# Gate and Up of two token tiles as seven products of 256 columns a pair of blocks, with sums of the weights kept in DRAM

## Chip, cores and metric

One core of one Trainium2 chip runs the whole kernel. The metric is the device time of one execution in microseconds (us); lower is better. TensorE (PE, with its weight loads shown as PEld), VectorE (DVE), ScalarE (ACT) and GpSimd (POOL) each run their own queue of instructions; SyncE (SP) issues nearly all transfers. Line numbers (L1059) are those of the kernel before.

## What is computed

x has 2048 tokens of 512 numbers. Both halves of the work start from the layer-normed x:

```
xn = layernorm(x)
s  = attention(xn)          # 32 heads of 16, causal window of 256 keys, then @ wo
h  = silu(xn @ w1) * (xn @ w3)     # 512 -> 1792, Gate and Up
g  = silu(h @ w2)                  # 1792 -> 512, Down
out = x + s * g
```

Results are wanted at nearly float32 accuracy. Every matrix is therefore scaled by a power of two and split into two float16 parts, high and low, and a product a @ b is computed as three: high x high, low x high, high x low.

## The kernel before

**Tiles.** Tokens go in four tiles of 512 (t = 0 to 3). The 1792 columns of w1 and w3 go in 14 blocks f of 128, in seven pairs j = (2j, 2j + 1). `X[t]` holds the normed tokens of a tile, turned so that the 512 features lie on the partitions in four pieces c, as XH (high) and XL (low).

**Gate and Up.** `gate_up(t, f)` makes Gate (k = 0, from w1) and Up (k = 1, from w3) of one block: for each k, 4 pieces x 3 products = 12 matmuls of 512 columns at L1059, added up in one PSUM bank. ACT takes tanh of Gate's bank (L1074), DVE multiplies it with Gate's bank (L1078, silu by way of tanh) and then with Up's bank (L1083). In tile 0 the weights are scaled and split as they come (`measure`, `split_pool`: two ACT instructions and four of POOL at L345 a weight) and their two parts are stored in `dW1`; later tiles load them from there (`load`), two blocks ahead.

**Down.** In tiles 0 and 1 h is split by ACT (L1092) and POOL (L339) and multiplied as it is (`down`, L1284). In tiles 2 and 3 Down already goes by Strassen's algorithm: `fold_first` and `fold_second` form sums of quarters of h (even and odd tokens by blocks 2j and 2j + 1) on POOL (L1116, L1117, L1125, L1140 to L1142) and ACT (L1114); `fold_down_piece` makes seven products of 256 columns (L1202), which ACT or DVE take out of PSUM (L1216, L1220); `unfold` adds them up to the four blocks of Down's result. The sums of w2 are made in tile 1 (`fold_weights`, L1014 to L1030) and kept in `dFold` (L1035).

**Attention.** 32 units (tile, group of 8 heads, half). Of each, `pass1` finds the maxima of the scores (PE L671, DVE L685), `pass2` computes scores again, adds masks (DVE L766), takes exp (ACT L769) and multiplies with the values (PE L787). A unit's rows are cut into five batches (`PLAN`).

**Order.** PE keeps the order in which the program issues; the other engines' queues are ordered by priority, with `urgent` ahead. `feed_forward` writes one list of dense pieces (Gate, Up, Down, loads, preparation of weights), each with a cost; `more` hands every unit its share, beside projections (`project`, L601), values (`value`, L567) and the output product (`total`, L1336). `spread` puts the dense pieces between the unit's batches in proportion to cost. `step` counts pieces and batches; `later(n, f)` runs f n steps on. A group of pieces that `opening` joins isn't parted by other dense pieces.

**Memory.** PSUM has four banks for scores, two for attention's results, and two, m0 and m1, for all dense products: `bank` gives them in turn. SBUF has 54 slots of 2 KB a partition; `take` gives the one that has been free longest, `give(..., after=n)` returns one, to be preferred from n steps on. Transfers go through SP's queue in the order of issue, and an instruction there waits for its data and its slot.

## Time and profile before

| | |
|---|---|
| median of 3 runs | 803.87 us |
| lowest and highest | 803.73 and 803.97 us |
| span of the profiled execution, first to last instruction | 801.8 us |
| instructions | 23974 |
| bytes read from and written to HBM | 91.23 and 36.57 MB |
| transfers "slot<-dW" of 256 KB | 98 |

The profile is of one execution, and of that execution it gives the span alone; the 2.07 us between it and the median lie before the first and after the last instruction, or between executions. In the profile's lists of groups a row gives line, engine, operation, what it writes and reads, shapes and count; after the first bar the engine's busy time in us and the mean duration of one in ns; after the second the idle time before, and what ended it. In a timeline a row gives start and length in us. Durations of PE's matmuls overlap: the next one starts before the one before has left the array, so pace is read from start to start. In rows of one line the three numbers are the shortest, median and longest duration in ns.

### The profile page before, as it was taken

How to read it: one execution, taken by the hardware profiler on the slowest of the kernel's cores; microseconds unless marked ns; L12 is line 12 of the kernel's file. 1: busy time of each engine (PE TensorE's matmuls, PEld its weight loads, DVE VectorE, ACT ScalarE, POOL GpSimd, SP SyncE). 2: the span in 40 equal slices, each digit the busy share in tenths (PEclk: the TensorE clock that was granted, in tenths of full speed). 3: DMA queues.
4: the chain of work that ended last, by engine and by line, in shares of the span. 5: the costliest groups of instructions: out<-in, count | busy, mean ns of one | idle time of the engine just before them, and what ended most of it. 6: DMA issues, size and time to landing. Idle time of an engine off the chain costs nothing.

```text
span 801.8 us, 23974 instructions
## 1 busy us (share of the span) xinstructions
PE 791.1 (99%) x9181; PEld 403.8 (50%) x9181; DVE 623.0 (78%) x2005; ACT 393.9 (49%) x592; POOL 381.2 (48%) x746
## 2 busy tenths in 40 slices
PE   8999999999999999999999999999999999999997
PEld 4443445444454444444445444466544744466465
DVE  8887889778797778787888887776678876874537
ACT  6989777744355544344443344344434334444411
POOL 2355657633229435365442546330446276650770
PEclk9999999999999999999999999999999999999999
DMA  9987654636666565657555733665453553334431
GB/s 281 245 258 238 196 185 144 248 111 208 173 215 189 169 210 144 214 148 258 130 194 173 213 114 101 177 173 157 137 159 87 159 157 110 89 117 134 129 94 56
DMA packets 109858, 134.18 MB, mean 167 GB/s; under 512 B 18928, under 2 KB 64944, under 8 KB 109744
## 3 DMA queue, kind: packets, MB, share of 16 engines
q1 hardware_dynamic: 109456, 132.13, 55.4%
q8 instruction: 72, 1.18, 0.6%
q10 hardware_dynamic: 288, 0.52, 0.2%
q14 instruction: 42, 0.34, 0.1%
HBM read 91.23 MB, written 36.57 MB: 159 GB/s over the span
## 4 chain that ended last, share of the span: by engine, by line
PE 80%; DVE 8%; DMA 4%; ACT 3%; issue 2%; POOL 1%; SPq 1%; DVEq 0%; ACTq 0%; POOLq 0%
PE m L1059 31%; PE po L787 9%; PE m L601 8%; PE m L1202 8%; PE m L1284 7%; PE s L759 5%; PE m L1336 4%; PE m L567 4%; PE s L671 3%; DMA slot<-in_B_w_dram 2%; DVE junk L685 2%; PE po L671 2%; ACT sqa L249 1%; DVE s L766 1%; POOL slot L345 1%
## 5 line engine op out<-in xcount | busy, mean ns | idle before, releaser
L1059 PE MATMUL m<-XH,slot 128*128 128x512 f16 x896 | 267.3, 380 | 1.1 <-DVE slot L1078 0.6
L769 ACT ACTIVATE pt<-s,es 128x1024 f32<-128x1024 f32 x152 | 167.6, 1112 | 178.7 <-DVE s L766 176.9
L1059 PEld LDWEIGHTS <-slot 128*128 128x128 f16 x1344 | 124.9, 98 | 155.6 <-issue 13.1
L1059 PE MATMUL m<-XL,slot 128*128 128x512 f16 x448 | 169.8, 379 | 0.0
L766 DVE TENSOR_TENSOR s<-s,MK 128x256 f32<-128x256 f32 (+2 forms) x280 | 118.7, 434 | 53.5 <-PE s L759 49.8
L685 DVE CUSTOM_DVE_ANT_0 junk<-s,MW 128x320 bf16<-128x320 f32 x276 | 133.9, 485 | 18.4 <-PE s L671 11.4
L339 POOL TENSOR_TENSOR slot<-slot,slot 128x256 f16<-128x256 f32 (+1 forms) x86 | 57.6, 692 | 128.8 <-ACT slot L1092 60.0
L345 POOL TENSOR_TENSOR slot<-slot,slot 128x128 f16<-128x128 f32 x168 | 68.9, 444 | 76.6 <-ACT slot L343 76.6
L685 DVE CUSTOM_DVE_ANT_0 junk<-po,MW 128x320 bf16<-128x320 f32 x172 | 83.4, 485 | 4.6
L1284 PE MATMUL m<-slot,slot 128*128 128x512 f16 x336 | 78.5, 380 | 1.1 <-DVE slot L1078 1.1
L787 PE MATMUL po<-pt,V 64*32 64x320 f32 (+4 forms) x2880 | 77.2, 342 | 0.1
L601 PE MATMUL m<-XH,slot 128*128 128x512 f16 x240 | 70.8, 380 | 0.5 <-DVE slot L1078 0.5
L1202 PE MATMUL m<-slot,slot 128*128 128x256 f16 x588 | 68.4, 273 | 0.0
L1074 ACT ACTIVATE slot<-m,sgs 128x512 f32<-128x512 f32 x56 | 38.3, 684 | 59.8 <-PE m L1059 59.7
L1117 POOL TENSOR_TENSOR slot<-slot,slot 128x256 f16<-128x256 f32 x98 | 64.6, 671 | 1.1
L1202 PEld LDWEIGHTS <-slot 128*128 128x128 f16 x588 | 56.2, 98 | 11.5 <-issue 2.8
L787 PEld LDWEIGHTS po<-pt,V 64*32 64x32 f32 x2880 | 50.4, 106 | 22.4 <-issue 0.8
L1078 DVE SCALAR_TENSOR_TENSOR slot<-slot,m 128x512 f32<-128x512 f32 x56 | 38.3, 684 | 28.9 <-ACT slot L1074 26.7
L759 PE MATMUL s<-qa,KA 50*64 50x320 f16 (+3 forms) x1472 | 58.3, 259 | 0.0
L601 PEld LDWEIGHTS <-slot 128*128 128x128 f16 x392 | 36.5, 98 | 42.6 <-issue 1.7
L759 PEld LDWEIGHTS <-KA 50*64 50x64 f16 x1472 | 30.1, 105 | 51.7 <-issue 32.8
L1284 PEld LDWEIGHTS <-slot 128*128 128x128 f16 x336 | 30.7, 98 | 39.2 <-issue 4.7
(194 smaller groups left out, 1131.5 us busy)
## 6 DMA issues: line engine op xcount, KB each, us to landing
slot<-dW SPq DMA_DIRECT2D x98, 256.0 KB
slot<-in_B_w_dram SPq DMA_DIRECT2D x56, 256.0 KB
slot<-dFold SPq DMA_DIRECT2D x48, 256.0 KB
dW<-slot SPq DMA_DIRECT2D x42, 256.0 KB
slot<-in_A_x_dram SPq DMA_DIRECT2D x30, 256.0 KB
KA<-dK SPq DMA_DIRECT2D x24, 288.0 KB
slot<-dWQ SPq DMA_DIRECT2D x24, 256.0 KB
qa<-dQ SPq DMA_DIRECT2D x30, 192.0 KB
```

What stands on the lines that cost most here:

```text
L339: op(out[:, c], a[:, c], b[:, c])
L345: nc.gpsimd.tensor_sub(lo[:, c:c + P], raw[:, c:c + P], hi[:, c:c + P])
L601: nc.tensor.matmul(cell["pp"][:, cols[n]], w[:, (a * NC + c) * P:(a * NC + c + 1) * P], b[:, c, cols[n]], start=n == 0 and (c, i) == parts ...
L685: lasts["maximum"] = nc.vector.tensor_tensor_reduce(out=junk[:, :n], in0=s[:, r, :n], in1=mask, scale=1.0, scalar=NEG, op0=ALU.add, op1=AL ...
L759: nc.tensor.matmul(s[64 * h:64 * h + 64, r, o:o + 64 * n], ka[rows, 2 * p + a, 64 * (m + 4):64 * (m + 5)], qa[rows, 2 * p + a, 64 * (m + k ...
L766: nc.vector.tensor_add(v, v, MK[:, kind, of:of + n, :].unsqueeze(1).to_broadcast([P, 2 * len(which), n, 64]))
L769: lasts["exp"] = nc.scalar.activation(pt, s, AF.Exp, scale=es)
L787: nc.tensor.matmul(cell["po"][32 * i:32 * i + 32, h, 64 * (m + k):64 * (m + k + n)], V[64 * h:64 * h + 64, (4 * t + m // 2) % VB, hd * VW: ...
L1059: nc.tensor.matmul(cell[k], w[:, (a * NC + c) * P:(a * NC + c + 1) * P], b[:, c, :], start=c == 0 and i == 0, stop=c == NC - 1 and i == 2)
L1117: nc.gpsimd.tensor_sub(lo, view, hi)
L1202: nc.tensor.matmul(cell["ps"][:, c], made[:, f:f + P], wj[:, g:g + 256], start=j == j0 and c == 0 and n == 0, stop=j == j1 - 1 and n == 2, ...
L1284: nc.tensor.matmul(ps, hh[:, a * TW + b * P:a * TW + (b + 1) * P], w[:, c * D:(c + 1) * D], start=f == f0 and i == 0, stop=f == f1 - 1 and ...
```

## The change

For tiles 2 and 3, Gate and Up of a pair of blocks are computed by Strassen's algorithm (in Winograd's form of seven products). The tokens' features are cut into halves d = 0, 1 (pieces c = 0, 1 and 2, 3), the tokens into halves of 256, the weights' columns into the two blocks. A product now has 256 columns and 256 features, and Gate and Up of it share one PSUM bank (columns 0 to 255 and 256 to 511): 12 matmuls of 256 columns.

- `quad(t, j)` replaces `gate_up` for a pair: p1, p2, p6, p5, p7, p3, p4, in this order. p1, p6, p5 and p3 add up in one bank, which `retained` keeps from other use meanwhile; after each, ACT copies its state to SBUF (`copied`). p2, and p7 with p4, use the other bank; DVE adds those to a copy (`added`). From each finished quarter `activated` makes half of h: tanh on ACT, a product on DVE, and the product with Up on POOL.
- `weight_sums(j)` makes four sums of blocks a pair and weight (POOL), splits them and stores them in `dSum`; it is started at seven places of tiles 1 and 2 (`QUAD_AT`). `token_sums(t)` makes the tokens' sums, kept in SBUF (`HALF`), at `HALVES_AT`.
- `load_quad` loads seven slots of 256 KB a pair, issued beside the products of the quad before (`LOADS`).
- `split_blocks` lays high and low parts of w1 and w3 out by feature halves, so that a half with both parts is one piece of `dW1`; `gate_up` reads that layout. `by_half` parts tokens by halves and not by parity.
- Scales: XS and the scale of h in tiles 2 and 3 (HF) are halved, copies are scaled by CS.
- Order: `arranged` places the other dense runs around a quad's four runs (p1 p2, p6, p5 p7, p3 p4), with one other run after p6; pieces marked `glued` aren't parted by batches. Of Down's products of the fold before at most seven runs (`LATE`) follow each quad. Projections of one group and the totals of tile 2 move by a unit.

```diff
-XS = 2.0**10
+XS = 2.0**9
+HF = 2.0**3
+CS = 2.0**-21
+LATE = 7
+QUAD_FROM = 2
+QUAD_AT = ((1, 2), (1, 4), (1, 7), (1, 10), (1, 13), (2, 1), (2, 2))
+HALVES_AT = {2: (1, 8), 3: (2, 5)}
...
-        open_bank[0] = b = 1 - open_bank[0]
+        open_bank[0] = b = 1 - (open_bank[0] if retained[0] is None else retained[0])
...
+    def weight_sums(j):
...
+        def sums(k):
+            a, b = (cell["raw"][i][k] for i in range(2))
+            add(b[:, r], b[:, l], b[:, r])
+            sub(b[:, l], a[:, l], b[:, l])
+            sub(a[:, l], b[:, r], a[:, l])
+            sub(a[:, r], a[:, r], a[:, l])
+
+        def cut(i, k):
+            raw = cell["raw"][i][k]
+            made = take(F16)
+            with behind_exp():
+                nc.scalar.copy(made[:, 0:512], raw)
+            halves(sub, made[:, 512:], raw, made[:, 0:512])
...
+                    nc.sync.dma_start(dSum[i, k, j], made)
...
+        def product(ps, w, x, first):
+            for k in range(2):
+                for c in range(2):
+                    for n, (a, b) in enumerate(((0, 0), (1, 0), (0, 1))):
+                        nc.tensor.matmul(ps[:, 256 * k:256 * k + 256], w(k, a, c), x(b, c),
+                                         start=first and k == 0 and c == 0 and n == 0,
+                                         stop=k == 1 and c == 1 and n == 2, skip_group_check=True)
+
+        def copied(ps):
+            made = take(F32)
+            with urgent():
+                lasts["exp"] = nc.scalar.activation(made, ps, AF.Copy, scale=CS)
+            return made
+
+        def added(ps, other):
+            with urgent():
+                lasts["emptied"] = nc.vector.scalar_tensor_tensor(other, ps, CS, other, op0=ALU.mult, op1=ALU.add)
+            return other
+
+        def activated(f, half, made, done_with=True):
...
+            nc.scalar.activation(h, made[:, 0:256], AF.Tanh, scale=sg_apart[:, f:f + 1])
+
+            def gated():
+                nc.vector.scalar_tensor_tensor(h, h, 1.0, made[:, 0:256], op0=ALU.add, op1=ALU.mult)
+                nc.gpsimd.tensor_mul(h, h, made[:, 256:512])
+                give(made, after=10)
+            later(1, gated)
...
+        def p6():
+            product(cell["a"], summed_up(0, 0), token_sum(1, 256), False)
+            cell["u2"] = copied(cell["a"])
+
+        def p5():
+            product(cell["a"], summed_up(1, 256), token_sum(0, 0), False)
+            cell["v5"] = copied(cell["a"])
+
+        def p7():
+            cell["b"] = bank([P, 512])
+            product(cell["b"], summed_up(1, 0), token_sum(0, 256), True)
+            give(QW[t, j, 5], QW[t, j, 6])
+            activated(o, 1, added(cell["b"], cell["v5"]))
+
+        def p3():
+            product(cell["a"], summed_up(0, 256), tokens(1, 256), False)
+            give(QW[t, j, 3], QW[t, j, 4])
+            retained[0] = None
+            activated(e, 1, copied(cell["a"]))
+
+        def p4():
+            product(cell["b"], plain(2), token_sum(1, 0), False)
...
+            activated(o, 0, added(cell["b"], cell["u2"]))
...
+            later(2, lambda: fold(e, fold_first))
+            later(3, lambda: fold(o, fold_second))
...
+            if t >= QUAD_FROM:
+                for j in range(FB // 2):
+                    pieces += sums_of(t, j)
+                    if j == 0 and t > 2:
+                        pieces += soon
+                    pieces += quad(t, j)
+                    some, late = late_of(late)
+                    pieces += some
...
-            for u, half in ((max(2 * k - 5 + (k == NG), 0), 1), (2 * k - 4, 0)):
+            for u, half in ((max(2 * k - 5 + (k in (NG, 3 * NG)), 0), 1), (2 * k - 4, 0)):
...
-        b = n % 8 - (2 if t < 3 else 3)
+        b = n % 8 - (2 if t < 3 else 4)
```

More of the change, by code (lines that the diff above doesn't have):

```diff
@@ new lines, in tile_block, with token_sums, both, sums @@
+    HALF = {}
+    def token_sums(t):
+        assert turned[t] == 4
+        xh, xl = X[t]
+        add, sub = nc.gpsimd.tensor_add, nc.gpsimd.tensor_sub
+        l, r = slice(0, 256), slice(256, 512)
+        whole = [take(F32) for _ in range(NC)]
+        HALF[t] = [None] * NC
+        def both(c):
+            halves(add, whole[c], xh[:, c, :], xl[:, c, :])
+        def sums(c):
+            a, b = whole[c], whole[2 + c]
+            sub(a[:, l], a[:, r], a[:, l])
+            sub(a[:, r], b[:, r], a[:, r])
+            sub(b[:, r], b[:, r], a[:, l])
+            sub(b[:, l], b[:, l], b[:, r])
+        def cut(c):
+            HALF[t][c] = made = take(F16)
+            with behind_exp():
+                nc.scalar.copy(made[:, 0:512], whole[c])
+            halves(sub, made[:, 512:], whole[c], made[:, 0:512])
+            give(whole[c], after=20)
+        n = 0
+        for f, cs in ((both, (0, 2, 1, 3)), (sums, (0, 1)), (cut, (0, 2, 1, 3))):
+            for c in cs:
+                later(n, lambda f=f, c=c: f(c))
+                n += 2
@@ L1376, in total_by_columns, with is_open, in_groups @@
         give(y, xr)
+    def is_open(pieces):
+        return bool(pieces) and hasattr(pieces[-1][1], "opens")
+    def in_groups(pieces):
+        groups = []
+        for piece in pieces:
+            if groups and is_open(groups[-1]):
+                groups[-1].append(piece)
+            else:
+                groups.append([piece])
+        return groups
     def feed_forward():
@@ L1447, in tile_block @@
     done = [0]
-    def is_open(pieces):
-        return bool(pieces) and hasattr(pieces[-1][1], "opens")
-    def in_groups(pieces):
-        groups = []
-        for piece in pieces:
-            if groups and is_open(groups[-1]):
-                groups[-1].append(piece)
-            else:
-                groups.append([piece])
-        return groups
     def more(want):
@@ L1508, in spread, with in_runs @@
+    def in_runs(dense):
+        runs = []
+        for piece in dense:
+            if runs and getattr(runs[-1][-1][1], "glued", False):
+                runs[-1].append(piece)
+            else:
+                runs.append([piece])
+        return runs
     def spread(made, dense):
         whole = sum(c for c, _ in dense) + sum(c for c, _ in made)
-        dense = list(dense)
+        dense = in_runs(dense)
         at = 0
@@ L1516, in spread @@
             at += cost
-            while dense and (at + dense[0][0] / 2 <= whole * (k + 1) / len(made) or dense[0][0] == 0):
-                c, piece = dense.pop(0)
+            while dense:
+                c = sum(c for c, _ in dense[0])
+                if c and at + c / 2 > whole * (k + 1) / len(made):
+                    break
                 at += c
-                piece()
-                if c:
-                    step()
-        run(dense)
+                run(dense.pop(0))
+        run([piece for r in dense for piece in r])
     def run(dense):
@@ L1663, in tile_block @@
         mine = more(want)
-        lists = in_groups(beside[n]), in_groups(mine)
+        head = next((i for i, (_, f) in enumerate(mine) if hasattr(f, "quad")), len(mine))
+        groups = in_groups(beside[n])
+        part_of = 0
+        if head == len(mine):
+            part_of = len(groups)
+        elif any(c for c, _ in mine[:head]):
+            part_of = round(len(groups) * sum(c for c, _ in mine[:head]) / sum(c for c, _ in mine))
+        lists = groups[:part_of], in_groups(mine[:head])
         both = sorted([((i + 0.5) / len(l), k, i) for k, l in enumerate(lists) for i in range(len(l))])
-        spread(batches(n, u, units[n + 2] if n + 2 < len(units) else None), [piece for _, k, i in both for piece in lists[k][i]])
+        dense = [piece for _, k, i in both for piece in lists[k][i]]
+        if head < len(mine):
+            dense += arranged([piece for g in groups[part_of:] for piece in g], mine[head:])
+        spread(batches(n, u, units[n + 2] if n + 2 < len(units) else None), dense)
         k = n // 2 + 2
```

218 lines of the change are left out of this document (208 added, 10 removed).

## Prediction

> **What bounds the kernel now.** I read the page's first part, then the busy times by stretch, then the costliest groups, then the waits.
>
> ```profile
> PE 791.1 (99%) x9181; PEld 403.8 (50%) x9181; DVE 623.0 (78%) x2005; ACT 393.9 (49%) x592; POOL 381.2 (48%) x746
> ...
> DMA  9987654636666565657555733665453553334431
> ...
> PE 80%; DVE 8%; DMA 4%; ACT 3%; issue 2%; POOL 1%; SPq 1%; DVEq 0%; ACTq 0%; POOLq 0%
> ...
> core 0: us, PE busy (x) PEld busy (x) DVE busy (x) ACT busy (x) POOL busy (x), PEclk, DMA share, GB/s
> 220.00:430.00 210.00, 209.78 (x2521) 99.32 (x2518) 170.93 (x534) 100.19 (x133) 105.32 (x190) 1.00 0.61 187
> 430.00:773.00 343.00, 342.38 (x4327) 184.20 (x4320) 249.00 (x753) 138.12 (x179) 162.75 (x276) 1.00 0.48 136
> ```
>
> TensorE (PE) is busy 791.1 of 801.8 us, at full clock in every stretch (1.00), and holds 80% of the chain. From 430 to 773 us, where Gate and Up of tiles 3 and 4 lie, it is idle for 343.00 - 342.38 = 0.62 us. So time is won only by giving PE less to do, and lost by any new wait of PE. VectorE (DVE) is at 73% there, ScalarE (ACT) at 40%, GpSimd (POOL) at 47%: none bounds, but PE's PSUM banks are emptied by DVE and ACT.
>
> **What goes, on PE.** A pair of blocks f, f+1 now takes 2 x 2 x 12 = 48 matmuls of 512 columns at L1059; after, seven products of 12 matmuls of 256 columns, 84. Durations overlap, so I take start to start, at the tail where nothing lies between:
>
> ```profile
> 768.07 0.60 PE L1059 MATMUL m<-XH,slot 128*128 128x512 f16 x2
> ...
> 773.04 0.38 PE L1059 MATMUL m<-XL,slot 128*128 128x512 f16 x1
> 773.26 13.92 PE L1202 MATMUL m<-slot,slot 128*128 128x256 f16 x126
> ```
>
> 24 matmuls of L1059 start from 768.07 to 773.04: 4.97 / 23 = 216 ns each. The 126 of L1202 (the Down products, also 256 columns, each with its own weights) take 13.92 us, of which the last one's 0.273 is pipeline: 13.65 / 125 = 109.2 ns. A pair: 48 x 0.216 = 10.37 us before, 84 x 0.1092 = 9.17 after, 1.20 less; 7 pairs x 2 tiles: **-16.8 us**. This is the whole gain; nothing else leaves PE. The new scales, halves in place of parities and the other layout of w1 and w3 in `split_blocks` keep the counts and shapes of instructions, and projections and totals put a unit later move PE's work without changing it: nothing, hidden as now by PE's other dense work.
>
> **What comes, beside PE.** Prices from the groups (mean ns after the busy time):
>
> ```profile
> L1078 DVE SCALAR_TENSOR_TENSOR slot<-slot,m 128x512 f32<-128x512 f32 x56 | 38.3, 684 | 28.9 <-ACT slot L1074 26.7 <-DMA rb<-de 2.0
> L1083 DVE SCALAR_TENSOR_TENSOR slot<-m,slot 128x512 f32<-128x512 f32 x56 | 38.5, 687 | 13.9 <-PE m L1059 13.6
> L1074 ACT ACTIVATE slot<-m,sgs 128x512 f32<-128x512 f32 x56 | 38.3, 684 | 59.8 <-PE m L1059 59.7
> L343 ACT CAST slot<-slot 128x512 f16<-128x512 f32 x42 | 25.0, 611 | 0.5
> L342 ACT ACTIVATE slot<-slot,pi 128x512 f32<-128x512 f32 x28 | 19.4, 714 | 1.7 <-DVE pi L302 1.7
> L1114 ACT CAST slot<-slot 128x256 f16<-128x256 f32 x42 | 15.6, 403 | 59.9 <-DVE slot L1083 59.9
> L1220 DVE SCALAR_TENSOR_TENSOR slot<-m,fd,slot 128x512 f32<-128x512 f32 x14 | 10.5, 748 | 7.0 <-PE m L1202 6.8
> L1140 POOL TENSOR_TENSOR slot<-slot,slot 128x256 f32<-128x256 f32 x14 | 10.2, 727 | 53.7 <-DVE slot L1083 44.7 <-DVE NM L704 9.0
> L1216 ACT ACTIVATE slot<-m,fd 128x512 f32<-128x512 f32 x14 | 9.6, 686 | 21.1 <-PE m L1202 16.0 <-issue 5.0
> L339 DVE TENSOR_TENSOR slot<-slot,slot 128x256 f32<-128x256 f32 x6 | 2.3, 416 | 0.0
> ...
> L1117 POOL TENSOR_TENSOR slot<-slot,slot 128x256 f16<-128x256 f32 x98 | 64.6, 671 | 1.1
> q1 hardware_dynamic: 109456, 132.13, 55.4%
> ```
>
> DVE, a pair: 2 x (684 + 687) = 2.74 us go; three additions out of PSUM at 748 (L1220) and four half products at 416 (the 256-wide row of L339) come: 3.91. That is +1.2 a pair, 16 us in all. ACT: 2 x 684 goes; four copies at 686 (L1216) and four half activations at 403 (L1114, 256 wide) come: +3.0 a pair, 42 us. POOL: four products at 727, 2.9 a pair, 41 us. The sums of w1 and w3, once a pair, in the second tile and the start of the third: ACT 4 x 714 + 4 x 611 = 5.3, POOL 8 x 727 + 8 x 671 = 11.2, seven times 37 and 78 us. The token sums, twice: POOL 16 x 727 + 8 x 671 = 17 us. From 430 to 773, less the 17 us: DVE 265 of 326 (81%), ACT some 58%, POOL some 71%. None is full, so I put the busy time itself at nothing; it is hidden by PE's own 326 us, and costs where it makes PE's banks come free late.
>
> Transfers: 28 loads and 28 stores of 256 KB for the sums, and 98 loads for 56 in tiles 3 and 4, 25.7 MB more. By the q1 row 132.13 MB took 55.4% of 801.8 us, 3.36 us a MB. About 14 MB fall between 220 and 430: the share there goes from 0.61 to 0.83. The DMA row stands at 9 tenths in its first slices, so that much can be had. A quad's weights are asked for one quad (over 20 us) ahead, so I put transfers at nothing. All are issued by SP, in order, and a store waiting for POOL's cut holds everything behind it, the attention's fetches too. The nearest case is the folded w2's store:
>
> ```profile
> SPq L1035 <- POOL slot L1030: 9.2, 2, 8.8
> ```
>
> It held SP once for 8.8 us, between 220 and 430, where PE lost 0.22 us in all. A longer hold is in the range's upper part.
>
> **Term 1, hand-overs of PSUM banks.** `bank` has two banks. Before, each is filled for 12 matmuls of 512 (2.6 us) while the other is emptied. In a quad, bank a goes p1, p6, p5, p3, and each product adds onto what the one before left, after ACT has copied it; bank b goes p2, other work, p7, p4. So the cover is one product: p6 waits for the copy of p1 behind p2 alone, p3 for that of p5 behind p7, the next piece for that of p3 behind p4 (ACT, three); the middle piece for the addition of p2 behind p6, p4 for that of p7 behind p3, p7 for the middle piece's emptying behind p5, p2 for the piece before p1 (DVE, mostly, four). p5, which needs the copy of p6, has the middle piece before it. That is seven a quad, 98. Behind each, PE holds all scores, projections and products that follow, and DVE and ACT wait for those.
>
> ```profile
> 427.46 0.38 PE L1059 MATMUL m<-XL,slot 128*128 128x512 f16 x1
> 428.47 0.69 DVE L1083 SCALAR_TENSOR_TENSOR slot<-m,slot 128x512 f32<-128x512 f32 x1
> ...
> L1083 DVE SCALAR_TENSOR_TENSOR slot<-m,slot x28: 678/689/693, 428.5 to 773.5; 128x512 f32<-128x512 f32 x28
> ...
>   PE m L1059: 9.2, 10
> ...
> L1074 ACT ACTIVATE slot<-m,sgs x27: 679/687/688, 446.4 to 770.9; 128x512 f32<-128x512 f32 x27
> ...
>   PE m L1059: 38.4, 19
> ...
> 791.77 0.74 DVE L1340 SCALAR_TENSOR_TENSOR slot<-m,us,slot 128x512 f32<-128x512 f32 x1
> 792.56 2.75 PE L1336 MATMUL m<-slot,slot 128*128 128x512 f16 x12 [0.20 <-DVE slot L1340]
> ...
> 429.06 0.64 PE L759 MATMUL s<-qa,KA 50*64 50x320 f16 x24
> ```
>
> From the end of a product's last matmul the next product covers 13 x 0.1092 - 0.273 = 1.15 us. PE starts 0.05 after DVE's end (791.77 + 0.74 to 792.56). So the emptying may start 1.15 - 0.05 - 0.75 = 0.35 us late on DVE, 0.41 on ACT (0.69). How late does it start? In tiles 3 and 4, 28 rows of L1083 and 14 of L1220 start 0.31 us after their last matmul on average (the first of them 428.47 - 427.84 = 0.63); DVE was found idle for 10 of the 28. 17 of the 42 pass 0.35 us, by 0.13 a case over all 42. ACT (L1074, L1216; idle for 19 of 27) has a mean of 0.15, an excess of 0.04. Bare: 3 x 0.04 + 4 x 0.13 = 0.64 us a quad, 9.0 in all. But attention's batches go between the runs of a quad, five a unit, some 80 over 14 quads, and a batch adds at least 0.6 us of cover (0.64 in the row). With 0.6 more the same 42 leave 0.01 and 0.02: 1.6 in all. With all delays doubled and no batch (0.13 and 0.42), 29. I take **+5**, near the middle of 1.6 and 9.0, since runs and batches are about equal in number but not always alternate.
>
> **Term 2, POOL in the second tile.** POOL's 105 of 210 us gets six pairs' sums and one tile's token sums, 84: 90%. What PE needs from it there is the low half of h for Down (L339):
>
> ```profile
> 255.03 0.69 DVE L1083 SCALAR_TENSOR_TENSOR slot<-m,slot 128x512 f32<-128x512 f32 x1 [0.38 <-PE m L1059]
> ...
> 259.38 1.30 POOL L339 TENSOR_TENSOR slot<-slot,slot 128x256 f16<-128x256 f32 x2
> ...
> 263.45 1.46 PE L1284 MATMUL m<-slot,slot 128*128 128x512 f16 x6
> ```
>
> h is ready at 255.72, its low half at 260.68, and PE starts that group at 263.45: 2.8 us to spare, with POOL starting on it 3.7 us after h. A block of sums of one weight is 4 x 727 = 2.9 us ahead in POOL's queue. Between nothing and 2.9 for each of four groups (11.6); I take **+1.5**, since the bulk is not urgent and can go behind.
>
> **Term 3, the tail.** After the last product h passes addition, activation, product on DVE and on POOL by halves, 0.75 + 0.40 + 0.42 + 0.73 = 2.3 us, where one DVE operation (0.69) led to the fold before:
>
> ```profile
> 774.23 0.73 POOL L1140 TENSOR_TENSOR slot<-slot,slot 128x256 f32<-128x256 f32 x1 [4.48 <-DVE slot L1083]
> ...
> 780.69 1.41 POOL L339 TENSOR_TENSOR on<-on,rb 128x256 f32<-128x256 f32 x2
> ```
>
> POOL begins 1.6 us later and has two or three half products and the first fold in front, so the operand of the third Down product comes about 1.3 us late, and the attention's last product (780.69) 3 us, which has about 2 of slack. From 0 to 4; I take **+1.5**.
>
> **Sum.** -16.8 + 5 + 1.5 + 1.5 = -8.8. Against the profiled execution: 801.8 - 8.8 = 793.0 us of span; the median shown, 803.87, is 2.07 above that span, so 795.1. I say **795.0**. About 0.2% (1.6 us) is what a measurement of this kernel can tell from no change.
>
> **Rivals.** *Nearly the whole gain* (22%): batches shelter all hand-overs (1.6), POOL's order costs nothing, tail 0.5: 803.87 - 14.7 = 789.2. For it: PE loses only 0.62 in 343 us with DVE at 73%. Against: every cover there is twice as long.
>
> *Given back* (12%): bare hand-overs with delays half longer, some 13, and terms 2 and 3: 803 to 804.
>
> *VectorE becomes the late one, slower* (21%). Place: the four hand-overs emptied by DVE, and the half product `gated`, whose two inputs both lie in SBUF. Rows of that kind:
>
> ```profile
> 217.80 1.30 POOL L339 TENSOR_TENSOR slot<-on,slot 128x256 f16<-128x256 f32 x2
> ...
> 218.65 1.00 DVE L251 CUSTOM_DVE_ANT_0 junk<-slot 128x512 bf16<-128x512 f32 x1
> ...
> L334 DVE SCALAR_TENSOR_TENSOR slot<-slot,sw,slot x12: 739/747/910, 11.4 to 79.3; 128x512 f16<-128x512 f32 x12
> ...
> L251 DVE CUSTOM_DVE_ANT_0 junk<-slot x10: 676/686/1005, 16.6 to 225.2; 128x512 bf16<-128x512 f32 x10
> ```
>
> Their longest are 163 and 319 ns over their medians; the longest, at 218.65, begins while POOL works through two instructions (217.80 to 219.10). With POOL at 71%, 56 half products held for some 0.2 that often put 8 us on DVE: 273 of 326, 84%; the ratio of its busy to its idle time goes from 2.6 to 5.2, and its queue's delays about double. At 0.2 us over 98 hand-overs, 19.6 us, with terms 2 and 3 the time is 803.87 - 16.8 + 22.6 = 809.7. It decides from 0.14 (13.8 + 3 = 16.8). Against it: before 430 us DVE ran at 81% (170.93 of 210) and PE lost 0.22 us, under the longer cover. [...]
>
> *The change doesn't do what it says* (3%): 256-column products run slower than 109 ns since each needs its weights, or a store holds SP till weights are late. Each 5 ns a matmul is 1176 x 5 = 5.9 us; 126 in a row at 109.2 speak against it.
>
> **Chances.** Forecast 42%; it stands for 791 to 802. The last rival's 3% fall evenly on the three outcomes. Faster: 42 + 22 + 1 = 65%; same: 12 + 1 = 13%; slower: 21 + 1 = 22%. Range 787.5 (the whole gain, 787.1, with 0.4 lost) to 807.0, inside the slow rival, which leaves out about 3% below and 15% above.
>
> **What would show it.** Products' matmuls 109 ns apart; PE's idle time between 430 and the end of the last quad, now 0.62 us, at about 5, ended by copies and additions of the quads (right), near 1.6 (first rival) or near 20 with DVE over 84% (third). PE waits at Down in the second tile for POOL: term 2. A gap of one to two us between the last quad and the last Down products: term 3. I am wrong if the quads' matmuls are further apart, or if PE waits for a transfer.

## The result, and the profile after

The changed kernel takes 912.09 us (median of 4 runs, 908.82 to 914.71) against 803.92 for the kernel before in the same comparison (803.73 to 804.30): 1.134 times as long, 95% interval 1.131 to 1.137. The forecast of 795.0 and its whole range are missed. The profiled execution has a span of 907.0 us, 105.2 more than before. Line numbers from here on are those of the changed kernel, unless another is named.

The page's busy times, its chain and its clock row:

```profile
PE 802.7 (88%) x9685; PEld 462.6 (51%) x9685; DVE 642.3 (71%) x2048; ACT 464.4 (51%) x740; POOL 535.3 (59%) x962
...
PE 20%; POOL 9%; DVE 6%; issue 4%; ACT 3%; DMA 3%; SPq 1%; DVEq 0%; POOLq 0%; ACTq 0%
...
PEclk9999999999999989999998898899999999999999
```

(The chain's shares add up to 47% only, so it breaks off, and nothing is built on it here.) By its matmuls' pace TensorE was to have 16.8 us less work, and yet it is busy 802.7 us, 11.6 more than before; and it is idle for 907.0 - 802.7 = 104.3 us, where it was idle for 801.8 - 791.1 = 10.7. So 93.6 us of the loss is idle time, and the rest is longer busy time: 11.6 + 16.8 = 28.4 us. The last row explains most of that: the granted clock, 1.00 in every stretch before, has 8s in it, and its mean over the run is 0.966. In the trace's record of the clock every piece is full or half. The half pieces add up to 61.4 us inside the span, and PE was busy for 42.1 of them; matmuls of 256 columns start 213 ns apart there and 109 elsewhere (medians), so the cost is some 21.0 (an estimate: half of 42.1). The other 7.4 weren't measured apart. A likely part of them: PE stops 82 times, 23 times before, and at each stop the end of the last matmul is overlapped by no next one (an estimate: 59 stops at 379 - 216 = 163 ns are 9.6 us).

Busy time by stretch (columns as before: PE, PEld, DVE, ACT, POOL, then the clock):

```profile
220.00:430.00 210.00, 190.24 (x2224) 88.72 (x2229) 149.36 (x470) 109.02 (x153) 148.84 (x245) 0.97 0.65 192
430.00:600.00 170.00, 130.19 (x1746) 78.86 (x1731) 109.05 (x324) 73.24 (x114) 106.62 (x174) 0.90 0.55 165
600.00:873.00 273.00, 244.32 (x3393) 175.24 (x3391) 176.90 (x526) 125.10 (x191) 162.28 (x258) 0.97 0.54 158
```

The loss begins in the second tile, which has the sums' preparation and not one quad: PE lost 0.22 us there before and now 210.00 - 190.24 = 19.8. The worst stretch, 430 to 600, has quads and the last of the preparation together: 39.8 us idle, clock 0.90. DVE, ACT and POOL are all less loaded there (64, 43 and 63%) than DVE alone was before (73%).

The waits (engine, line, what it waited for; total, times, longest), first of the compute engines, then of SP's queue:

```profile
ACT slot L1135 <- POOL slot L1440: 55.6, 23, 5.2
PEld L618 <- DMA slot<-dWQ: 41.6, 9, 11.8
PE m L1414 <- ACT slot L1421: 19.0, 11, 6.4
```
```profile
SPq L1591 <- POOL slot L347: 13.5, 5, 10.5
SPq L1389 <- POOL slot L1440: 11.3, 4, 6.1
SPq L1387 <- PE m L1414: 7.6, 5, 3.8
```

Two chains stand behind these rows. **SP's queue.** The biggest wait of PE is for `dWQ`, the weights of the attention's projections (L618), which the change doesn't touch. The timelines of SP, POOL and PE about the longest case (start, length; SP's rows give when a transfer was issued):

```profile
554.58 0.46 SPq L1328 DMA_DIRECT2D dSum<-slot  x1
555.09 0.43 SPq L1387 DMA_DIRECT2D slot<-dW  x1
566.07 0.35 SPq L1591 DMA_DIRECT2D out_dram<-slot  x1
...
567.49 0.90 SPq L653 DMA_DIRECT2D slot<-dWQ  x2
...
562.69 0.74 POOL L1137 CAST slot<-slot 128x256 f16<-128x256 f32 x2
563.39 1.29 POOL L1138 TENSOR_TENSOR slot<-slot,slot 128x256 f16<-128x256 f32 x2
564.64 1.40 POOL L347 TENSOR_TENSOR slot<-slot,slot 128x256 f32<-128x256 f32 x2
...
559.02 0.31 PE L688 MATMUL s<-KA,qa 48*64 48x320 f16 x4
570.82 1.03 PE L618 MATMUL m<-XH,slot 128*128 128x512 f16 x2 [11.49 <-DMA slot<-dWQ]
571.65 0.63 PE L618 MATMUL m<-XL,slot 128*128 128x512 f16 x1
...
573.96 0.38 PE L618 MATMUL m<-XL,slot 128*128 128x512 f16 x1
```

After 555.5 us SP issues nothing until 566.07: there stands the store of a result (L1591), whose last addition is POOL's (L347, 564.64 to 566.04), and POOL comes to it only after folds, half products and sums. (It is the 10.5 us, the longest, of the row for L1591.) Behind the store wait two transfers, and then the two loads of `dWQ`, issued at 567.49. PE, which needs them, stands from 559.33 to 570.82. A store of a finished tile holds up the weights of an unrelated product. And when PE comes back, a matmul of 512 columns takes 0.63 us at 571.65 and 0.38 at 573.96: the clock had been halved meanwhile (by the trace's record at 563.46). The loads of the quads' weights hold SP in the same way, by L1389 for a slot that POOL has still to read, and by L1387 for one that PE is reading.

**ACT's queue.** The timelines of ACT and PE about another stop, at 682 us:

```profile
678.68 0.61 ACT L1370 CAST slot<-slot 128x512 f16<-128x512 f32 x1
682.39 0.40 ACT L1135 CAST slot<-slot 128x256 f16<-128x256 f32 x1 [3.09 <-POOL slot L1440]
682.70 0.50 ACT L1436 ACTIVATE slot<-slot,sga 128x256 f32<-128x256 f32 x1
683.11 1.09 ACT L786 ACTIVATE pt<-s,es 128x1024 f32<-128x1024 f32 x1
684.11 0.58 ACT L1421 ACTIVATE slot<-m 128x512 f32<-128x512 f32 x1
...
680.11 1.48 PE L1414 MATMUL m<-slot,slot 128*128 128x256 f16 x12
684.74 2.78 PE L1414 MATMUL m<-slot,slot 128*128 128x256 f16 x24 [3.15 <-ACT slot L1421]
```

The first instruction of the fold of h (L1135, a cast) reached the head of ACT's queue 3.09 us before POOL had finished the half product it reads (L1440). Behind it stand an activation, an exp and only then the copy of a PSUM bank (L1421), on which PE's next product waits for 3.15 us. ACT is busy for 46% of 600 to 873 us, but nothing in its queue passed that cast: the three behind it began at 682.70, 683.11 and 684.11. Altogether it stood at that cast for 55.6 us. Both chains are read from one case each; the runs below ask how much each is worth.

### The profile page after: what moved, and what is told of

It is laid out like the page before. It is cut to its first block, busy times and chain, and to the rows that moved or that the text cites. A ratio compares the mean times of both kernels' runs of the same rounds, so it can differ in the third digit from the quotient of the medians.

```text
span 907.0 us, 25623 instructions
## 1 busy us (share of the span) xinstructions
PE 802.7 (88%) x9685; PEld 462.6 (51%) x9685; DVE 642.3 (71%) x2048; ACT 464.4 (51%) x740; POOL 535.3 (59%) x962
## 5 line engine op out<-in xcount | busy, mean ns | idle before, releaser
L786 ACT ACTIVATE pt<-s,es 128x1024 f32<-128x1024 f32 x152 | 167.4, 1112 | 171.2 <-DVE s L783 163.7
L347 POOL TENSOR_TENSOR slot<-slot,slot 128x256 f16<-128x256 f32 (+1 forms) x158 | 105.2, 693 | 102.2 <-ACT slot L1113 47.2
L702 DVE CUSTOM_DVE_ANT_0 junk<-s,MW 128x320 bf16<-128x320 f32 x276 | 134.0, 485 | 29.9 <-PE s L688 22.4
L1414 PEld LDWEIGHTS <-slot 128*128 128x128 f16 x1176 | 115.3, 100 | 49.8 <-issue 30.5
L1080 PE MATMUL m<-XH,slot 128*128 128x512 f16 x448 | 133.7, 380 | 0.6 <-DVE slot L639 0.3
L618 PE MATMUL m<-XH,slot 128*128 128x512 f16 x240 | 77.4, 410 | 41.0 <-DMA slot<-dWQ 38.0
L1080 PEld LDWEIGHTS <-slot 128*128 128x128 f16 x672 | 62.1, 98 | 77.9 <-issue 6.7
L1414 PE MATMUL m<-slot,slot 128*128 128x256 f16 x672 | 84.4, 280 | 10.7 <-ACT slot L1421 6.9
L702 DVE CUSTOM_DVE_ANT_0 junk<-po,MW 128x320 bf16<-128x320 f32 x172 | 83.7, 487 | 4.7
L1080 PE MATMUL m<-XL,slot 128*128 128x512 f16 x224 | 84.9, 379 | 0.0
L618 PEld LDWEIGHTS <-slot 128*128 128x128 f16 x392 | 37.9, 103 | 91.0 <-DMA slot<-dWQ 41.6
L1440 POOL TENSOR_TENSOR slot<-slot,slot 128x256 f32<-128x256 f32 x56 | 41.5, 741 | 67.6 <-DVE slot L1439 36.9
L1223 PE MATMUL m<-slot,slot 128*128 128x256 f16 x588 | 69.7, 276 | 7.1 <-ACT slot L1237 2.9
L363 POOL TENSOR_TENSOR slot<-slot,slot 128x128 f16<-128x128 f32 x112 | 46.8, 452 | 47.8 <-DMA dQ<-slot 26.4
L1138 POOL TENSOR_TENSOR slot<-slot,slot 128x256 f16<-128x256 f32 x98 | 66.9, 692 | 11.7 <-ACT slot L1135 10.5
L1414 PE MATMUL m<-XH,slot 128*128 128x256 f16 x336 | 58.8, 279 | 13.1 <-ACT slot L1421 12.1
L1223 PEld LDWEIGHTS <-slot 128*128 128x128 f16 x588 | 56.5, 99 | 18.9 <-issue 8.9
L804 PEld LDWEIGHTS po<-pt,V 64*32 64x32 f32 x2880 | 52.4, 107 | 22.4 <-issue 2.9
```

What stands on the lines that cost most here:

```text
L347: op(out[:, c], a[:, c], b[:, c])
L618: nc.tensor.matmul(cell["pp"][:, cols[n]], w[:, (a * NC + c) * P:(a * NC + c + 1) * P], b[:, c, cols[n]], start=n == 0 and (c, i) == parts ...
L702: lasts["maximum"] = nc.vector.tensor_tensor_reduce(out=junk[:, :n], in0=s[:, r, :n], in1=mask, scale=1.0, scalar=NEG, op0=ALU.add, op1=AL ...
L786: lasts["exp"] = nc.scalar.activation(pt, s, AF.Exp, scale=es)
L804: nc.tensor.matmul(cell["po"][32 * i:32 * i + 32, h, 64 * (m + k):64 * (m + k + n)], V[64 * h:64 * h + 64, (4 * t + m // 2) % VB, hd * VW: ...
L1080: nc.tensor.matmul(cell[k], w[:, at:at + P], b[:, c, :], start=c == 0 and i == 0, stop=c == NC - 1 and i == 2)
```

## The experiments

Seventeen kernels were run, each beside the kernel before (803.9 to 804.9 in all comparisons). The expectations call the theories by letters: **Q**, queues run in order and SP or ACT stands at an instruction that waits for GpSimd; **S**, SBUF slots are short, so a load or a copy gets one that is still in use; **H**, hand-overs of PSUM banks, each covered by one product of 1.15 us only; **A**, of Q the part on ACT. Others are explained where they come. Times are medians; PE's idle time is the span less PE's busy time of the page, 10.7 us before.

| kernel | us | ratio, 95% interval | PE idle |
|---|---|---|---|
| changed kernel | 912.1 | 1.131 to 1.137 | 104.3 |
| e1 `dWQ` loaded earlier | 924.3 | 1.146 to 1.153 | 115.7 |
| e2 half product on DVE | 890.6 | 1.104 to 1.111 | 87.7 |
| e3 weights' sums not computed | 886.6 | 1.099 to 1.106 | 85.8 |
| e6 preparation moved | 901.0 | 1.115 to 1.125 | 100.1 |
| e7 e6 with e2 | 885.6 | 1.091 to 1.110 | 90.8 |
| e11 fold later | 903.8 | 1.121 to 1.127 | 92.0 |
| e4 preparation, no quads | 855.0 | 1.060 to 1.066 | 47.3 |
| e12 order and layout alone | 805.6 | 1.001 to 1.003 | 12.5 |
| e13 the same with e4's slots held | 817.0 | 1.009 to 1.024 | 19.6 |
| e8 e4 without the sums' transfers | 843.5 | 1.046 to 1.052 | 38.0 |
| e9 e4 without POOL's sums | 835.9 | 1.035 to 1.043 | 34.3 |
| e5 before, with 44 slots | 830.7 | 1.028 to 1.037 | 30.0 |
| e10 before, 84 more transfers | 804.0 | 0.999 to 1.001 | 10.7 |
| e14 quads, weights' sums left out | 845.0 | 1.046 to 1.056 | 54.9 |
| e15 the same, slots kept | 855.1 | 1.060 to 1.067 | 63.6 |
| e16 e14, half product on DVE | 826.9 | 1.025 to 1.031 | 40.5 |
| e17 e14, bank copies on DVE | 841.2 | 1.043 to 1.049 | 49.5 |

### First look: one cause at a time out of the changed kernel

**e1**, the loads of `dWQ` a unit earlier; **e2**, the half product on VectorE; **e3**, POOL's sums and low halves left out (another output); **e4**, all preparation but Gate and Up as before the change (the last two sums and tile 3's token sums start at corresponding places, as the list counts blocks there and not pairs; of e4 the main line is shown).

```diff
-                if u == n + 1 and tiles[k][0]:                                  # e1
+                if u == n + 2 and tiles[k][0]:
-                nc.gpsimd.tensor_mul(h, h, made[:, 256:512])                    # e2
+                nc.vector.tensor_mul(h, h, made[:, 256:512])
-            halves(sub, made[:, 512:], raw, made[:, 0:512])                     # e3
+                nc.scalar.copy(made[:, 512:], raw)
-                later(n, lambda k=k: sums(k))
+                pass
-            if t >= QUAD_FROM:                                                  # e4
+            if t >= NT:
```

> Edit: the loads of the projections' weights (slot<-dWQ) are issued one unit earlier. Theory Q (a late GpSimd holds SyncE's in-order queue, and the projection's weights behind it come late): PE's waits for slot<-dWQ, 41.6 us, fall below 10, the half-clock stretches that follow them shrink, time 850 to 875. Rival H (hand-overs of PSUM banks inside the quads): the dWQ waits are a symptom that moves elsewhere, time stays within 905 to 915. Rival D (transfers are simply too many for the DMA engines): weights still land late, within 900 to 915.

> Edit: the product of activated Gate with Up goes from GpSimd to VectorE (56 instructions of 0.73 us off GpSimd, 56 of some 0.42 onto VectorE). Theory Q: GpSimd's busy time falls by 41 us, SyncE's holds in tiles 3 and 4 shorten, the dWQ waits after 430 us (about 27 us) halve: 875 to 895. Rival H: VectorE is more loaded and empties banks later: 912 to 925. Rival D: 908 to 914.

> Left out: the sums of w1 and w3 and their low halves on GpSimd (56 additions of 0.73 us and 56 subtractions of 0.67, 78 us); ScalarE writes the stored slot's second half instead, so the output differs; loads, stores and quads stay. Theory Q: GpSimd is no longer full from 268 to 330 us, the dWQ waits between 250 and 420 us (14.5 us with their half clock) go, some of the later ones too: 880 to 895. Rival H: within 908 to 914, since the quads are untouched. Rival D: within 908 to 914, since the transfers are untouched.

> Edit: all sums of weights and tokens are made and stored, but Gate and Up of tiles 3 and 4 are computed as before (512 columns, no quads, no quad loads). Theory Q: the second tile's share of the loss stays: 815 to 835, with GpSimd full around 270 to 330 us and waits for dWQ there. Rival H: the quads hold all of the loss: 803 to 808.

**e1** took 924.3 us, 12 more than the changed kernel, against all three expectations. Of e1, the waits for `dWQ` are gone, but:

```profile
PE m L1414 <- ACT slot L1421: 36.8, 16, 17.5
```

and in the timelines of ACT and SP:

```profile
488.62 0.60 ACT L1421 ACTIVATE slot<-m 128x512 f32<-128x512 f32 x1 [14.15 <-DMA dK<-slot]
...
482.28 0.39 SPq L645 DMA_DIRECT2D dK<-slot  x1
```

A copy of a bank now waited 14.15 us, and not for PE: for the slot it writes to, which a store to `dK` had still to read; SP came to that store at 482.28. PE stood 17.5 us. So to load one thing earlier takes a slot and a place in SP's queue from another; the wait moves.

**e2** (890.6) and **e3** (886.6) took the times that Q forecast, 21 and 25 us won by 34 and 76 us less work on an engine that is 59% busy. But they did not win them where Q said. PE's waits for `dWQ`, 41.6 us in the changed kernel, were to halve after 430 us in e2 and to go between 250 and 420 in e3. In e2, then in e3:

```profile
PEld L618 <- DMA slot<-dWQ: 39.9, 9, 9.7
```
```profile
PEld L618 <- DMA slot<-dWQ: 34.6, 10, 8.1
```

In e2 they hardly move, and in e3 11.3 of the 14.4 us before 420 stay. What falls in both is PE's idle time that an exp of ACT ended, from 14.1 us to 6.9 and 7.6. So much of the gain came by ACT's queue and not by SP's, and POOL's arithmetic isn't all of the preparation's cost. D (too many transfers as such) forecast 908 to 914 for both, with the transfers untouched, and missed. **e4** is the surprise: 855.0, above both forecasts. Without one quad, half of the loss is there, 51 us.

### What the preparation costs

**e5**: the kernel before with fewer slots. **e8** and **e9**: e4 without the sums' 28 loads and 28 stores (ACT fills the slots from a constant instead), and e4 with e3's edit. **e10**: the kernel before with 84 more issues on SP. **e12**: scales, layout and moved order, without sums or quads. **e13**: e12 with slots taken and given back at the steps of e4 and nothing done in them.

```diff
-SLOTS = 54                                                                      # e5
+SLOTS = 44
-                lasts["load"] = nc.sync.dma_start(a[k], dW1[f, k])              # e10
+                for c in (slice(0, 512), slice(512, 1024)):
+                    lasts["load"] = nc.sync.dma_start(a[k][:, c], dW1[f, k][:, c])
```

> Edit: the kernel before, unchanged work, with 44 of its 54 SBUF slots. Counted in the program's order of takes and gives, 90 of 628 slots are then taken before the step from which their last reader was planned to be done (9 with 54 slots; 211 of 798 in the changed kernel). Theory S (too few slots: loads and stores in SyncE's in-order queue wait for the readers of the slot they reuse, and what stands behind them, the projections' weights first, comes late): 830 to 880, with PE waiting for slot<-dWQ and half-clock stretches, as in the changed kernel. Rival Q (GpSimd is overloaded by the new sums): no new work on GpSimd, 802 to 808. Rival H (hand-overs inside quads): no quads, 802 to 808.

> e4_prep (all sums made, Gate and Up as before) with the sums' transfers left out: 28 loads of w1 and w3 and 28 stores to dSum; ScalarE fills the four slots from a constant instead, GpSimd's and ScalarE's arithmetic and the slots stay, and nothing reads the sums there. Theory I (SyncE's one in-order queue is nearly full before the change: 937 transfers at 0.52 us of issue each, 65 in every 50 us of the first 450, and each further one delays all behind it): 808 to 820, dWQ waits below 5 us. Rival Q (GpSimd's arithmetic is what is late): 840 to 856. Theory S (slots): 825 to 845.

> e4_prep with GpSimd's arithmetic of the weights' sums left out (sums and low halves; ScalarE copies instead, so dSum holds other numbers, which nothing reads), its loads and stores kept. Theory I: 830 to 850. Rival Q: 804 to 815. Theory S: 825 to 845.

> Edit: the kernel before, with each of the 84 loads of w1's and w3's parts (slot<-dW) issued as two of half the columns: same bytes, slots, engines and order, 84 more issues on SyncE, some 44 us of its time. Theory I: 820 to 850 with waits for dWQ and dW. Rivals Q, S and H: 803 to 808.

> e4_prep without any sums: only the new layout of w1 and w3, the halves in place of parities, the scales and the moved projections and totals stay; no weights' or tokens' sums, no quads. Theories S, Q and P (below) alike: 803 to 807, early takes as before (9 of 628). Rival O (the moved projections and totals, or the new layout, are at fault): 815 to 840.

> e12_bare plus the slots of the sums and nothing else: they are taken and given back at the same steps as in e4_prep, but nothing is loaded, computed or stored in them. Theory S (the slots that the sums hold make other tiles reuse slots before their last readers are done): 822 to 838, with dWQ waits, which is most of what e8_nodma and e9_noarith have in common. Rival P (the ScalarE and GpSimd work itself delays what other engines need): 803 to 808.

e12 and e10 acquit two suspects: order and layout cost 1.5 us, and SP's time to issue nothing. The rest is shared. Slots alone, between e12 and e13, cost 11.4 us (some 5 to 18, as e13's two runs are 5 us apart); the transfers, between e4 and e8, 11.5; POOL's arithmetic, between e4 and e9, 19.0. With the 1.5 that is 43.4 of the 51; the other 7 are work left in all of these (ACT's, the token sums) or act only together. The sum is a rough one: slots were added to e12 alone, the others taken out of e4 one at a time, and parts that act together needn't add up. No theory comes out whole. e8 is far above I's range, e9 above Q's; both lie in S's, but e13, with slots alone, lies below S's 822 to 838 and above P's 803 to 808. e5 shows slots from another side: with ten fewer and nothing else, the kernel before is 26 us slower, by the same wait. PE's wait for `dWQ` in e4, then in e5 (whose line is L601):

```profile
PEld L618 <- DMA slot<-dWQ: 22.1, 6, 5.5
```
```profile
PEld L601 <- DMA slot<-dWQ: 15.8, 4, 6.4
```

So free slots are part of what lets SP's queue run ahead of PE. A count of the programs says how much of it the change uses: in the kernel before `take` had to hand out 9 of 628 slots ahead of the step that `give` had asked for, in the changed kernel 211 of 798.

### What the quads cost by themselves

**e14**: quads, with the weights' sums left out (loads fetch parts of `dW1` in their place; another output). **e15**: e14 with the first pair's weights kept for all pairs, 91 loads fewer. **e16**: e14 with e2's edit. **e17**: e14 with the four copies of a pair on VectorE. The same edits on the full kernel: **e11**, the fold emitted six steps later.

```diff
-            if (t, at) in sums_at:                                              # e14
+            if False:
-            lasts["load"] = nc.sync.dma_start(made, dSum[(i - 3) // 2, (i - 3) % 2, j])
+            lasts["load"] = nc.sync.dma_start(made, dW1[2 * j + (i - 3) // 2, (i - 3) % 2])
+        if (t, j) != (QUAD_FROM, 0):                                            # e15
+            QW[t, j, i] = QW[QUAD_FROM, 0, i]
+            return
-                lasts["exp"] = nc.scalar.activation(made, ps, AF.Copy, scale=CS)    # e17
+                lasts["emptied"] = nc.vector.tensor_scalar(made, ps, CS, None, op0=ALU.mult)
-            later(2, lambda: fold(e, fold_first))                               # e11, both folds
+            wait = 2 if any(j == j1 - 1 for _, j1 in FOLDS) else 8
+            later(wait, lambda: fold(e, fold_first))
```

> The changed kernel without the weights' sums: quads load parts of w1 and w3 from dW in their place (same bytes and issues, other numbers, so the output differs); token sums and quads stay. If the two halves of the loss add up: 912 - 51 = 861, between 852 and 870, with PE's waits before 430 us below 5 us. If the second half is fed by the first (rival F: delays of the second tile carry over): below 845.

> e14_noprep with the seven weight slots of the first quad kept for all 14 (91 loads fewer, slots from some 10 to 7; the output differs). Theory S for tiles 3 and 4: 10 to 25 us below e14_noprep. Rival H or A (hand-overs and ScalarE's queue held by GpSimd): within 5 us of e14_noprep.

> Edit: the changed kernel with the folds of h emitted six steps later (but for the last pair of each group of four or three). In tiles 3 and 4 ScalarE's copy of a bank (L1421), for which PE waits 21 us, stands behind ScalarE's cast of h (L1135), which waits 56 us for GpSimd's half product. Theory A (ScalarE's in-order queue, held by GpSimd, is what makes the hand-overs late): PE's waits for L1421 fall below 10 us, 885 to 902. Rival H (the cover of one product is too short as such): the waits for L1421 stay at 18 to 24, 905 to 914.

> The seven-product pairs without the weights' sums (their operands are loaded from dW1, so the output is another), as in e14 (845.0 us), and the half product h x Up on VectorE in place of GpSimd. In e14 ScalarE stood 63.6 us in front of the fold's cast, waiting for that product on GpSimd, with PE waiting 16.4 us for the copies of PSUM banks and 10.5 us for exps behind it. Theory A (ScalarE's in-order queue, held by GpSimd, makes the bank copies and exps late): the hold falls under 25 us, PE's idle time from 49 to 20-30 us, the time to 818-832. Rival H (the copies are late whoever makes the product, since a bank is covered by one product only): PE's idle time stays above 42 us, 838-850 us.

> As e14 (845.0 us; weights' sums left out, another output), and the four copies a pair of a PSUM bank made by VectorE, not by ScalarE; the half product stays on GpSimd and the hold on ScalarE with it. Theory A: the copies no longer stand behind the fold's cast, so PE's 16.4 us for them fall to under 8 (by VectorE), 828-840 us, while the exps' 10.5 us stay. Rival H: the wait moves whole to VectorE, which gets 56 x 0.7 = 39 us more work; 842-858 us.

e14 took 845.0, below the 852 to 870 of two halves that add up and at the edge of F's: the quads (with the token sums and the 1.5 of order and layout) are 41 us slower by themselves, 58 if the 16.8 they save is added. Its waits, then those of e16:

```profile
PEld L618 <- DMA slot<-dWQ: 0.6, 1, 0.6
ACT slot L1135 <- POOL slot L1440: 63.6, 25, 5.4
PE m L1414 <- ACT slot L1421: 12.4, 11, 3.2
```
```profile
PEld L618 <- DMA slot<-dWQ: 1.1, 1, 1.1
ACT slot L1135 <- DVE slot L1440: 19.6, 16, 2.2
PE m L1414 <- ACT slot L1421: 12.3, 12, 2.3
```

The wait for `dWQ` is gone from both: it belongs to the preparation. Keeping the weights (e15) doesn't help; that kernel is 10 us slower than e14, against both forecasts, and PE's wait for the copies rises from 12.4 to 23.5 us (L1417 and L1424 there). Fewer loads thus don't cure the quads; why the kernel got slower wasn't followed, so e15 says nothing sure of their slots. e16, one instruction moved from POOL to DVE, wins 18 us: the hold on ACT falls from 63.6 to 19.6 us, PE's idle time from 54.9 to 40.5; the time is within A's forecast. But the idle time stays above A's 20 to 30, and the wait for the copies hardly falls, from 12.4 to 12.3 us. e17 says the same from the other side (841.2, between both forecasts): with DVE in place of ACT for the copies, and the hold still there,

```profile
PE m L1414 <- DVE slot L1421: 12.5, 12, 3.2
```

the wait only changes its name. So a half product on POOL, and the hold that it makes, is worth 18 us (PE's idle time that an exp ended falls from 10.6 to 3.1 us). Of the 29.8 us by which e16's idle time is still above that of before, 15.0 were ended by a copy or an addition of the quads: that much goes to the thin cover, as far as waits tell, for no run had a longer cover. What a hand-over without the long hold looks like, in the timelines of ACT and PE of e16:

```profile
614.84 0.51 ACT L1436 ACTIVATE slot<-slot,sga 128x256 f32<-128x256 f32 x1 [0.19 <-DVE slot L1426]
615.81 1.11 ACT L786 ACTIVATE pt<-s,es 128x1024 f32<-128x1024 f32 x1 [0.47 <-DVE s L783]
616.82 0.59 ACT L1421 ACTIVATE slot<-m 128x512 f32<-128x512 f32 x1
...
613.65 1.49 PE L1414 MATMUL m<-slot,slot 128*128 128x256 f16 x12
617.46 4.16 PE L1414 MATMUL m<-slot,slot 128*128 128x256 f16 x24 [2.32 <-ACT slot L1421]
```

The exp waited 0.47 us for its mask, then ran 1.11, and the copy behind it came out 2.32 us late for PE. An exp takes 1.11 us (mean of L786), so one that has just begun in front of a copy takes nearly the whole cover of 1.15 us. e11 didn't take the hold away (56.0 us, as in the changed kernel), so its 903.8, at the border of the two forecasts, decides nothing.

### Whether the preparation fits elsewhere

**e6** moves the sums of the weights into the first tile and the quads' loads to the end of the quad before; **e7** adds e2's edit.

```diff
-QUAD_AT = ((1, 2), (1, 4), (1, 7), (1, 10), (1, 13), (2, 1), (2, 2))
-HALVES_AT = {2: (1, 8), 3: (2, 5)}
+QUAD_AT = ((0, 6), (0, 7), (0, 9), (0, 10), (0, 12), (0, 13), (1, 1))
+HALVES_AT = {2: (1, 11), 3: (2, 5)}
-    LOADS = ((0,), (1,), (3, 4), (5, 6), (), (), (2,))
+    LOADS = ((), (), (), (0,), (1,), (3, 4), (5, 6, 2))
```

> Edit: same work as the changed kernel; the weights' sums are started in the second half of tile 1, where slots are free (QUAD_AT from (0, 6) to (1, 1)), tile 3's token sums at (1, 11), and a quad's weights are loaded in the second half of the quad before. Early takes fall from 211 to 89 of 798, the rest after 400 us. Theory S: the waits between 200 and 430 us (20 us with their half clock some 27) nearly go, those after shrink: 845 to 875. Rival Q: GpSimd's load moves out of 250 to 350 us, but its sum is the same: 880 to 900. Rival H: 905 to 914.

> Edit: e6_moved with the product of activated Gate with Up on VectorE. Theory S: GpSimd's readers give slots back earlier in tiles 3 and 4: 10 to 20 us below e6_moved. Rival Q: 20 or more below. Rival H: 0 to 10 above e6_moved, since VectorE empties banks later.

901.0 and 885.6 us. e6 misses all three forecasts (S's 845 to 875 by 26 us); e7 is 15 us below it, as S said. The second tile's waits nearly go, and some 36 us of idle time appear between 100 and 250, where the kernel before had 1. The loss travels with the work. None of the seventeen beats the kernel before.

## Why the prediction failed

**The term of -16.8 us held,** as a pace: the twelve matmuls of a product take 1.48 us (row at 680.11), 11 x 109 + 273 ns. It was paid for many times over by stops.

**Busy times were nearly right.** DVE was to get 16 us more and got 19.3, POOL 153 (41 + 78 + 2 x 17) and got 154.1, ACT 79 and got 70.5. What each operation does in the changed kernel (line, engine; shortest, median, longest in ns):

```profile
L1421 ACT ACTIVATE slot<-m x56: 573/589/599, 456.1 to 872.7; 128x512 f32<-128x512 f32 x56
L1436 ACT ACTIVATE slot<-slot,sga x56: 492/508/519, 458.1 to 877.4; 128x256 f32<-128x256 f32 x56
L1439 DVE SCALAR_TENSOR_TENSOR slot<-slot,slot x56: 355/503/981, 459.0 to 877.9; 128x256 f32<-128x256 f32 x56
L1440 POOL TENSOR_TENSOR slot<-slot,slot x56: 716/725/915, 459.6 to 881.1; 128x256 f32<-128x256 f32 x56
```

A copy is cheaper than priced (589 against 686), a half activation dearer (508 against 403).

**The first step that failed: "none is full, so I put the busy time itself at nothing".** It argued from shares of busy time. POOL's share rose from 48 to 59% only, but what counted here is how long its queue was when something in it was needed: between 540 and 566 us it is busy for 24.9 of 26, and a result's last addition stands in it behind sums nobody needs yet. From 430 to 600 us, with the three engines at 43 to 64%, PE was idle for 39.8 us.

**The second, and the larger: "I put transfers at nothing".** It had seen that a store waiting for POOL holds everything behind it on SP, took one hold of 8.8 us that had cost nothing as the measure, and let a longer one go into the range's upper part. It didn't ask why that hold had cost nothing. The likely answer is that the loads behind it were early enough because slots were free; e5, with ten fewer slots, and e13 speak for it. The change takes that lead away three ways at once: more waiting stores, more slots held, a later POOL. Where the prediction had nothing, PE waited 41.6 us for loads of `dWQ`, the largest of its waits; the kernel before has none. The preparation alone costs 51 us (e4), and next to the quads 67 (912 less e14's 845); it isn't all transfers, as 19 of the 51 go with POOL's arithmetic (e9), the first step. In the second tile, where **term 2** looked for POOL's low half of h at Down (+1.5), no stop of PE was for that; 13.4 of its 19.8 us were for `dWQ`. The rival that named "a store holds SP till weights are late" was thus right in kind; it shared 3% with another mishap and had no price.

**The third: term 1, hand-overs, +5.** The cover was right; the delays were taken from rows of the kernel before. The prediction allowed a copy on ACT to start 0.41 us after a product's last matmul and an addition on DVE 0.35. The mean excess over that (copies after p1, p5 and p3, and the three additions of a quad, 42 of each, every one taken with its own product), and PE's idle time that a copy or an addition ended:

```
                 copies (ACT)   additions (DVE)   14 x (3 copies + 4 additions)   PE's idle time
predicted        0.04 us        0.13 us            9.0 us                          5 (less by batches)
e14              0.71           0.50              58                              18.5
e16              0.49           0.34              39                              15.0
```

So the shelter by batches was there, as most of the lateness did not reach PE; what was mis-sized is the lateness, 4 to 18 times as large in e14, and the term should have been some 18 and not 5. The same copies on ACT were 0.71 us late in e14 and 0.49 in e16, with one instruction moved: in these runs the delay went with what stood in the queue and not with the engine alone, and the quads put work there that waits. The rest of the 44.2 us by which e14's idle time is above that of before has no term in the prediction: 10.6 were ended by exps, behind the hold on ACT, 4.2 by the maxima of the scores (L702), the others by many small cases.

**VectorE as the late one** (the rival on the slower side) is not it: DVE is busy 65% of 430 to 873 us, and of PE's idle time in the changed kernel an addition of a quad ended 1.6 us only. Its price was right, though: of the 56 half products at L1439 the 14 that no POOL instruction overlaps take 417 ns on average, the 42 others 609. **The tail** (term 3, 1.5, from 0 to 4) had the right mechanism and too small a size: after the last quad PE stops for 1.43, 0.74 and 0.92 us among the last Down products, first for an addition and then for POOL's sums, and for 1.42 in the output products, 4.5 us in all, against 0.2 before.

**The half clock** wasn't in the prediction as a cost at all: its price, some 21 of the 28.4 us of longer busy time, came only with stops of PE: the step of 3.41 us before each of the twelve half pieces has 2.04 us or more of idle time (last section).

Not settled: how the preparation and the quads raise each other's cost (51 + 41 is 92, and the loss is 108), and the 7 us of e4 that no single edit removed. Which of the nine waits for `dWQ` go back to POOL and which to slots was followed for the longest one only.

## What to carry to other kernels

Work put on engines with free time wasn't free here (ACT, busy for 46% of 600 to 873 us, stood 3.09 us at one cast with a copy for PE behind it): list what will stand behind each new instruction that waits, on SP and ACT too, and how early the transfers behind it are now; count the free buffers as well (ten fewer cost the kernel before 26 us, with PE waiting for `dWQ`). When a product is cut into smaller ones, the cover of a bank shrinks with it (here from 12 x 216 ns, 2.6 us, to 1.15), and the emptier's queue must be shorter than that cover: here a single exp of 1.1 us in front of the copy was too much for 1.15. Before a saving of 2% is spent on such a change, measure its preparation alone, with the results unused: here e4 would have shown half of the loss at once.

## What the runs showed of the hardware

- **A stop of PE can be paid twice.** In the rows at 571.65 and 573.96 a matmul takes 0.63 us and then 0.38. In the trace's record of the clock the half pieces are 3.4, 6.8 or 10.2 us long, 61.4 us in all against none inside the span before; matmuls of 512 columns start 427 ns apart in them and 216 outside (medians). All twelve pieces begin on one grid of 3.41 us, and the step of the grid before each has 2.04 us or more of idle time; at full clock, no step with up to 1.96 us was followed by one. So after the stop of 2.04 us from 457.78, within one step, the clock was half, and after the one of 3.15 us at 681.59, which falls into two steps (1.34 and 1.82 us), it wasn't.
- **SP's issue time was no limit.** e10 has 84 more transfers and the same time to 0.1% (804.04 us against 804.16).
- **DVE with two SBUF inputs beside POOL** takes 192 ns longer on average (L1439, 417 to 609). The longest, 981 ns, began 34 ns after a POOL instruction and ended 282 ns after that one's end. Three that began 155 to 162 ns ahead of a POOL instruction took 413 to 418, as if alone, and the POOL instructions 842 to 849 where their median is 725. So in these four cases whichever came first went on, and the other paid.
